# Loads on a second queue, a shorter warm-up, a later scale and earlier weight loads in a conditioned transformer block

## The chip, the cores and the metric

The kernel runs on one core of one Trainium2 chip. The metric is the device time of one execution in microseconds; a kernel's time is the median of its runs.

## The reference, cut to what matters

One block on 2048 tokens of width 640, all in float32. A conditioning vector `c` gives six modulation vectors (shift, scale and gate, for attention and for the MLP). The input is normalised and modulated, goes through linear attention with 32 heads of width 20, and is added back through a gate; the sum is normalised and modulated again, goes through an MLP of width 1728 with a squared ReLU, and is added back through the second gate.

```python
mod = (_silu(c) @ w_mod).reshape(c.shape[0], 6, 1, -1)
sa, ca, ga, sb, cb, gb = (mod[:, 0], mod[:, 1], mod[:, 2], mod[:, 3], mod[:, 4], mod[:, 5])
h = _layernorm(x, axis=-1) * (1 + ca) + sa
x = x + ga * _A_ref(h, A_wqkv, A_w_phi, A_wo)
h = _layernorm(x, axis=-1) * (1 + cb) + sb
x = x + gb * _B_ref(h, B_w1, B_b1, B_w2, B_b2)
...
# in _A_ref, per head: features are softmax(q w_phi) and softmax(-q w_phi), the same for k
o = num / den          # phi_q (phi_k^T v)  over  phi_q (phi_k^T 1)
# in _B_ref
r = jnp.where(h > zero, h, zero); h = r * r
```

## The kernel before, in words

**Numbers in two parts.** Every matmul operand is held as a high and a low part: ACT copies the value into a rounded format (the high part), DVE subtracts that from the value (the low part, `lo`, line 80), and `three` (line 76) makes three matmuls of each product. A weight therefore passes through three steps: a raw tile is loaded, ACT makes its high part, DVE its low part.

**The start.** The head matrices of `w_phi` lie in a block matrix `bd`. `fold` (line 231) multiplies the raw k and q weights by it, 12 matmul instructions for each of five pieces `d` of k and then of q. While the loads are under way, PE runs `WARM` matmuls on a tile of ones (lines 551 to 553); a float32 matmul is two instructions in the trace. The first two tokens' tiles (`XB[0]`) are normalised by `stats` and `scale`, transposed, modulated by `out0` (`t_out`, line 336: two ACT steps and one DVE step), and used by `k_step` (line 539), five steps `d` of 12 matmuls; `mod_rows2`, `mod_sb` and `mod_cols2` work out the modulation columns between them. Within this loop (lines 579 to 591) the next pair of tiles, `XB[1]`, gets its `stats` at `d == 1` and its `scale` (line 502, two ACT steps) at `d == 2`. After the loop ACT makes the high part of the first v weight (`v_hi(0)`) and empties the four PSUM banks of the k products (`to_sb`), which the q products then take.

**The middle.** For token tiles 2 to 13 the loop at line 641 makes k, q, v, the exponentials and the running k-v sums, with preparations (`side`) between. The q exponentials go out to DRAM and come back.

**The output projection and the preparation of the MLP.** Lines 1284 to 1332 run the first four pairs of token tiles through `do_wo`; the steps in `EXTRA` normalise the results (`ln2`), send them to DRAM in blocks (`blocks`, on ACT's queue, tile `xn`), bring them back (`back`, on SP's queue, tile `sb`) and transpose them on DVE (`turn`). The 28 MLP weight pieces stand in one list, `preps`, that runs through w1 and w2 by turns. Three counters go through it: `p_load` issues the raw load, `p_hi` is ACT's step and `p_lo` is DVE's. Nine loads are issued ahead of the MLP.

**The MLP.** `group(0)` to `group(3)` (line 1543) take 512 tokens each. Step `f` of 14 computes `up_mm` for piece `f` of w1, ACT's ReLU (line 1375) and square, both parts, and, two steps later, `down` with piece `f` of w2. In group 0 the weights are still being prepared: at step `f` PE does `up_mm(f)`; then come the low parts of the weights whose high parts came a step before; then the ReLU; then the normalisation of the next group's pairs 2 and 3 in pieces, with `back(2)` at step 5 and `back(3)` at step 7; then `p_hi` up to piece 2f+7; then `down(f - 2)`; and last `p_load` up to piece 2f+11. POOL and DVE meanwhile work on the late q tiles (`late_load`, `late_out`).

**What sets the order.** Between `manual_schedule` and its end, the engines named there (in this stretch PE, DVE and ACT) keep the order in which the program writes the instructions. SP's queue is not among them for this stretch: a planner puts SP's transfers in order by its own simulated clock, taking an instruction as soon as its inputs and a slot for its output are there, and the chip then runs that queue strictly in that order. `behind_sp` (line 1152) ties `back` to a place behind the last SP transfer that the program has written so far. The loop over tiles 2 to 13 is put in order by the planner on all engines.

**Slots.** Tiles with the same tag share a fixed number of slots (line 40). A tile gets its slot when its first writer is put in order, and tiles of one tag get theirs in the order in which the program writes their first writers. Raw pieces 0 to 8 are in tag `s1` (3 slots); later ones go by turns into `s1`, `s2` (2 slots) and `s4` (5 slots). The s4 slots were last held by the tiles `ept` of the output projection. One s4 slot goes to `LATE["b"]` (trace name `etl`), first written by `late_out(8)` at step 4 of group 0. The prepared pieces are in tag `w` (21 slots) or in the ring; the ring's 'w' slots for pieces 16 and 17 (w1 piece 9, w2 piece 7) were last held by the normalised tiles `xm` of pairs 2 and 3, which are free when `blocks` has written them to DRAM.

Of the kernel before, what the change touches and what calls it, by code (L numbers as in the profile page):

```python
# [22 lines left out]
NC = D // P  # L23
NF = 14
# [8 lines left out]
FIRST = 4  # L33
NTA = 2 * FIRST
RAWQ = NTA + 3
WARM = 14
APART = 256 + 16
SIDES = 3
DIRECT = range(6)
# [4 lines left out]
def kernel(  # L44
# [19 lines left out]
    nc = tc.nc  # L64
# [11 lines left out]
    def three(ah, al, bh, bl):  # L76
        return [(ah, bh), (ah, bl), (al, bh)]
# [16 lines left out]
    def tok2(tag, name):  # L94
        return mem.tile([P, 2, D], F32, tag=tag, name=name, bufs=BUFS[tag])

    def row(tag, name):
        return mem.tile([P, D], F32, tag=tag, name=name, bufs=BUFS[tag])
# [4 lines left out]
    def wslot(name, tag="w", pool=None):  # L103
        t = tok2(tag, name) if pool is None else pool.tile([P, 2, D], F32, tag=tag, name=name)
        return t.bitcast(F32R)
# [11 lines left out]
    def pj(name):  # L117
        return [psA.tile([P, 512], F32, tag="pj", name=f"{name}_{h}", bufs=4) for h in range(2)]

    def tp(name):  # L120
        return psA.tile([P, 512], F32, tag="tp", name=name)
# [16 lines left out]
    c_t = const.tile([P, NC], F32, name="c_t")  # L138
# [41 lines left out]
    first = tc.manual_schedule(engines={ET_.PE, ET_.DVE, ET_.Activation, ET_.Pool, ET_.SP})  # L180
    first.__enter__()

    nc.sync.dma_start(c_t, c)
    bd_t = row("s4", "bd_t")
    nc.sync.dma_start(bd_t, bd)
    raw, WM, RV, XB = {}, {}, {}, {}

    def load_raw(nm, w5, w1):
        raw[nm] = [tok2("w", f"raw_{nm}{i}") for i in range(3)]
        nc.sync.dma_start(raw[nm][2][:40, 1], w1)  # L190
        for d in range(NC):
            nc.sync.dma_start(raw[nm][d // 2][:, d % 2], w5[d * P : (d + 1) * P])

    def load_x(j):
        XB[j] = tok2("x", f"xb{j}")
        nc.sync.dma_start(XB[j], x[256 * j : 256 * j + 256].rearrange("(i p) d -> p i d", p=P))
# [31 lines left out]

    W = {}

    def fold(nm, d):

        w = wslot(f"w{nm}{d}")
        W[nm, d] = w
        p = pj(f"fold{nm}{d}")
# [132 lines left out]
    def proj(nm, t, cuts=((0, 320), (320, 640)), between=None):  # L368
# [3 lines left out]
        for h, (a, b) in enumerate(cuts):  # L372
# [3 lines left out]
            for d in range(NC):  # L376
                w = W[nm, d]
                terms += three(HT[j][:, d, 0, s], HT[j][:, d, 1, s], w[:, 0, a:b], w[:, 1, a:b])
# [144 lines left out]
    def mod_sb(d):  # L523
        t = MR[d, "sb"] = row("s1", f"msb{d}")[:, :P]
        nc.scalar.activation(t, MR[d][:, :P], AF.Identity, bias=plus[:, 0:1])
# [13 lines left out]
    def k_step(d):  # L539
        w = W["k", d]  # L540
        for t in range(2):
            s = slice(t * P, (t + 1) * P)
            for h in range(2):
                a, b = h * HALF, (h + 1) * HALF
                mm(PP[t][h][:, :HALF], three(HT[0][:, d, 0, s], HT[0][:, d, 1, s], w[:, 0, a:b], w[:, 1, a:b]),
                   first=(d == 0), last=(d == NC - 1))

    def out0(d):
        t_out(cols_a, HT[0], d, "a0", TR[d])

    warm = tp("warm")
    for i in range(WARM):
        nc.tensor.matmul(warm[:, :P], ones, ones, start=True, stop=True)
# [25 lines left out]
    for d in range(NC):  # L579
        if d + 1 < NC:  # L580
            mod_cols2(d + 1)
            out0(d + 1)
        if d + 2 < NC:
            mod_rows2(d + 2)
        k_step(d)
        if d + 2 < NC:
            mod_sb(d + 2)
        if d == 1:
            n1 = stats(XB[1], "a1")
        if d == 2:  # L590
            scale(XB[1], *n1)

    def v_hi(d):
        W["v", d] = wslot(f"wv{d}")
        nc.scalar.activation(W["v", d][:, 0], RV[d], AF.Copy)

# [266 lines left out]
    def late_exp():  # L863
        if "exp" in LATE:
            exps(ET[LATE.pop("exp")])
# [184 lines left out]

    W1, W2 = {}, {}

    def prep_load(k, f, w):
        n = FS[f]
        W = W1 if k == "1" else W2
        if k == "1":
            w = w.rearrange("p s (k n) -> p s k n", k=NC)
        W[f] = w
        i = preps.index((k, f))
        raw = row(("s1", "s2", "s4")[i % 3] if i > 8 else "s1", f"rw{k}_{f}")  # L1060
        if k == "1":
            raw = raw.rearrange("p (k n) -> p k n", k=NC)
        for r in range(P // n):
            if k == "1":
                nc.sync.dma_start(raw[:, :, r * n : r * n + n], w1[:, f * P : f * P + n].rearrange("(k p) n -> p k n", p=P))
            else:
                nc.sync.dma_start(raw[r * n : r * n + n], w2[f * P : f * P + n])
        RAW[k, f] = raw
# [1 line left out]
    RAW = {}  # L1070

    def prep_hi(k, f):
        w = (W1 if k == "1" else W2)[f]
        nc.scalar.activation(w[:, 0], RAW[k, f], AF.Copy)  # L1074

    def prep_lo(k, f):
# [18 lines left out]
    places = []  # L1095
    todo = {"load": list(preps), "hi": list(preps), "lo": list(preps)}

    def p_load(n=1):
        for _ in range(n):
            if todo["load"]:  # L1100
                k, f = todo["load"].pop(0)
                prep_load(k, f, places.pop(0)(f"w{k}_{f}"))

    def p_hi(n=1):
        for _ in range(n):
# [178 lines left out]
    for j in range(FIRST):  # L1284
        nxt = j + 1 < FIRST
        b, c = 2 * j + 5, 2 * j + 6
# [256 lines left out]
    def group(g):  # L1543
# [5 lines left out]
        for f in range(NF):  # L1549
            if nxt:  # L1550
                if f == 1 and not early:
                    load_x1(a)
                if f == 4 and not early:
                    load_x1(b)
                if f == (2 if early else 3):
                    lns.append([0, a, ln2(a)])
                if f == (4 if early else 7):
                    lns.append([0, b, ln2(b)])
                if f == 8:
                    fa_new()  # L1560
                    turn(a)
            if g == 0:
                if f == 0:
                    up_start(g, 2, 2)
                elif f > 1:
                    up_mm(g, f)
            elif g == FIRST // 2:
                if f == 0:
                    up_start(g, 4, 3)
                elif f == 2:  # L1570
                    up_mm(g, 4)
                elif f > 4:
                    up_mm(g, f)
            else:
                up_mm(g, f)
            if nxt and f == 11:
                turn(b)
                affine(range(NC))
            if f == (6 if g else 11):
                residual(g)  # L1580
            if f == 9 and g:
                add_b2(g)
            if g == 0:
                if f == 1:
                    late_slots()
                    for t in range(2):
                        late_load(NTA + t)
                    late_list()
                p_lo(len(todo["lo"]) - len(todo["hi"]))
                if 3 <= f < NF - 1:  # L1590
                    fill((3.5, 3.5, 3.5, 3.5, 3.0, 1.0, 0.0, 2.0, 1.0, 2.0)[f - 3])
            elif early:
                if f == 4:
                    late_blocks(4)
                    last_row("s1", 6)
                if f in (6, 7):
                    late_turn(4, ("q0", "q1") if f == 6 else None, LAST[4], (range(5), range(5, 11))[f - 6])
                if f == 8:
                    late_blocks(5)
                if f == 12:  # L1600
                    kv2_load()
                    late_wo(range(3))
                if f:
                    fill(3.4 if f in (6, 7, 9) else 5.2)
                if f == NF - 1:
                    assert not FILL, FILL
            if not more and f:
                round2(g, f)
            if f == 0 and g in (0, FIRST // 2):
                up_relu(g, 0)  # L1610
                up_relu(g, 1)
            if f == 2 and g == FIRST // 2:
                up_relu(g, 2)
                up_relu(g, 3)
            if g != FIRST // 2 or f != 3:
                up_out(g, f)
            if g == FIRST // 2 and f == 2:
                up_out(g, 3)
            if g and (more or f == 0):
                round2(g, f)  # L1620
            late_exp()
            for n in lns:
                n[0] += 1
                for _ in range(1 + (n[0] == 3)):
                    next(n[2], None)
                if n[0] == 4:
                    back(n[1])
            if g == 0:
                p_hi(2 * f + 7 - (2 * NF - len(todo["hi"])))
            if f == NF - 1 and nxt:  # L1630
                split2(range(NC))
            if f >= LAG:
                down(g, f - LAG)
            if g == 0:
                p_load(2 * f + 11 - (2 * NF - len(todo["load"])))
            else:
                ring_loads(g, f, FIRST // 2 if early else NGR)
        if g == 0:
# [94 lines left out]
```

## Time and profile before

| | us |
|---|---|
| median of 3 runs | 790.95 |
| lowest, highest run | 790.09, 791.35 |
| profiled execution | 790.26 |
| its span, first to last instruction | 788.6 |
| PE busy (matmul) | 777.0 |
| DVE busy | 553.8 |
| ACT busy | 403.0 |
| POOL busy | 76.5 |

Times in the trace count from the start of the span. In a timeline a row gives start and length in us, then engine, source line, operation, output and inputs, shape and count; the bracket gives the engine's idle time before the row and what ended it. A list of waits gives the total, the number of waits and the longest. SPq and ACTq are the issue of a DMA by that engine's queue; the transfer itself lands later. A table by windows gives, for each stretch, its length, the busy time of each engine with the number of instructions, then the granted clock, the busy share of the DMA engines and GB/s.

### The profile page before, as it was taken

The numbers are of one execution on the slowest core, as the hardware profiler recorded it, in microseconds if no ns is written. First come the engines' busy times: TensorE is split into PE (matmuls) and PEld (weight loads), VectorE is DVE, ScalarE is ACT, GpSimd is POOL, SyncE is SP. The second block draws the span as 40 slices with busy tenths as digits, with TensorE's granted clock in tenths as the row PEclk, the third lists the DMA queues.
The fourth block names the chain that finished last, engine by engine and source line by source line (L and its number), as shares of the span: only waits on it lengthen the run. The fifth ranks groups of instructions, "written<-read, shape, count | busy, mean of one in ns | idle before, by whom it ended". The sixth has DMA issues, their size and how long they took to land.

```text
span 788.6 us, 13327 instructions
## 1 busy us (share of the span) xinstructions
PE 777.0 (99%) x5171; PEld 717.4 (91%) x5171; DVE 553.8 (70%) x917; ACT 403.0 (51%) x789; POOL 76.5 (10%) x181
## 2 busy tenths in 40 slices
PE   9999999999999999999989999999999999999997
PEld 8899999999998988898979989999899999989997
DVE  4498999999766488664869699966945343575544
ACT  4667585655734344655938354531265644433221
POOL 3002020000000022201323000100010001000000
PEclk9999999999999999999999999999999999999999
DMA  8713248234121253567798747995779755145121
GB/s 329 265 36 132 101 163 278 90 140 152 54 84 34 84 185 137 167 188 243 245 350 293 249 165 265 282 330 201 206 234 343 274 169 166 51 150 200 34 84 67
DMA packets 76437, 142.31 MB, mean 180 GB/s; under 512 B 12718, under 2 KB 37422, under 8 KB 76374
## 3 DMA queue, kind: packets, MB, share of 16 engines
q1 hardware_dynamic: 69382, 117.74, 45.5%
q0 software_dynamic: 4096, 16.78, 5.6%
q10 hardware_dynamic: 2896, 6.94, 2.3%
q8 instruction: 40, 0.66, 0.3%
q14 instruction: 23, 0.19, 0.1%
HBM read 98.40 MB, written 42.93 MB: 179 GB/s over the span
## 4 chain that ended last, share of the span: by engine, by line
PE 80%; DVE 7%; DMA 5%; ACT 4%; POOL 2%; issue 1%; SPq 0%; ACTq 0%; DVEq 0%; POOLq 0%
PE up L70 20%; PE acc L70 13%; PE pv L70 9%; PE acr L70 8%; PE pk L70 8%; PE pq L70 8%; PE pwo L70 7%; PE kvp L415 3%; DMA xn<-xm 2%; DVE dn L813 2%; DVE scr L811 1%; DMA rw<-in_w 1%; DVE ezb L832 1%; PE ta L325 1%; DMA raw_k<-in_wk 1%
## 5 line engine op out<-in xcount | busy, mean ns | idle before, releaser
L70 PE MATMUL up<-h,w 128*128 128x512 f32 (+1 forms) x910 | 198.3, 371 | 2.9 <-ACT r L1375 2.7
L70 PEld LDWEIGHTS up<-h,w 128*128 128x128 f32 x910 | 155.7, 188 | 31.1 <-ACT r L1375 3.1
L70 PE MATMUL acc<-w,r2t 128*128 128x384 f32 x656 | 151.0, 336 | 0.1
L70 PE MATMUL acr<-w,r2t 128*128 128x256 f32 x656 | 112.8, 279 | 0.0
L70 PEld LDWEIGHTS acc<-w,r2t 128*128 128x128 f32 x656 | 107.5, 188 | 4.6 <-DVE r2t L80 0.4
L70 PEld LDWEIGHTS acr<-w,r2t 128*128 128x128 f32 x656 | 105.6, 188 | 0.0
L70 PE MATMUL pk<-wk,hT 128*128 128x320 f32 x480 | 79.8, 313 | 1.5 <-ACT hT L340 0.9
L70 PE MATMUL pwo<-wo,ot 128*128 128x320 f32 (+1 forms) x512 | 79.5, 313 | 0.1
L70 PE MATMUL pv<-wv,hT 128*128 128x360 f32 (+1 forms) x480 | 77.7, 311 | 0.0
L70 PEld LDWEIGHTS pwo<-wo,ot 128*128 128x128 f32 (+1 forms) x512 | 75.7, 188 | 1.1 <-DVE xm L1043 0.4
L70 PE MATMUL pq<-wq,hT 128*128 128x320 f32 x480 | 76.4, 314 | 0.1
L70 PEld LDWEIGHTS pk<-wk,hT 128*128 128x128 f32 x480 | 71.5, 188 | 3.7 <-ACT hT L340 1.4
L70 PEld LDWEIGHTS pv<-wv,hT 128*128 128x128 f32 x480 | 72.6, 188 | 0.3
L70 PEld LDWEIGHTS pq<-wq,hT 128*128 128x128 f32 x480 | 70.6, 188 | 1.6 <-ACT k L391 0.6
L1375 ACT ACTIVATE r<-up,b_t 128x512 f32<-128x512 f32 x52 | 35.0, 679 | 68.1 <-PE up L70 60.1
L80 DVE TENSOR_TENSOR r2t<-r,r2t 128x512 fp32r<-128x512 f32 (+1 forms) x56 | 38.4, 685 | 34.9 <-ACT r2t L1387 32.1
L80 DVE TENSOR_TENSOR w<-rw,w 128x640 fp32r<-128x640 f32 (+2 forms) x42 | 33.2, 814 | 28.3 <-ACT w L1074 16.9
L1386 DVE TENSOR_TENSOR r<-r 128x512 f32<-128x512 f32 x26 | 17.9, 690 | 47.1 <-ACT r L1375 47.1
L1387 ACT ACTIVATE r2t<-r 128x512 fp32r<-128x512 f32 x52 | 32.9, 633 | 22.4 <-DVE r L1386 21.6
L1477 ACT ACTIVATE w<-rw 128x640 fp32r<-128x640 f32 x42 | 30.6, 730 | 26.3 <-DVE rw L1476 24.1
L338 ACT ACTIVATE hfa<-ta,cols_a 128x256 f32<-128x256 f32 x30 | 17.0, 565 | 28.7 <-PE ta L325 28.6
L1074 ACT ACTIVATE w<-rw 128x640 fp32r<-128x640 f32 x28 | 19.4, 727 | 18.9 <-DMA xn<-xm 10.7
(241 smaller groups left out, 1079.7 us busy)
## 6 DMA issues: line engine op xcount, KB each, us to landing
rw<-in_w SPq DMA_DIRECT2D x65, 320.0 KB, 4.4
w<-w2d SPq DMA_DIRECT2D x28, 320.0 KB, 5.0
w<-w1d SPq DMA_DIRECT2D x12, 640.0 KB, 4.5
esp<-eq SPq DMA_DIRECT2D x11, 640.0 KB, 3.6
wm<-in_w_mod SPq DMA_DIRECT2D x20, 320.0 KB, 3.6
xb<-in_x SPq DMA_DIRECT2D x8, 640.0 KB, 4.1
el<-esp SPq DMA_DIRECT2D x8, 640.0 KB, 4.0
xx<-in_x SPq DMA_DIRECT2D x16, 320.0 KB, 3.5
```

What stands on the lines that cost most here:

```text
L70: nc.tensor.matmul(o, a, b, start=first and i == 0, stop=last and i == len(terms) - 1, skip_group_check=skip,)
L80: (eng or nc.vector).tensor_tensor(out_lo, full, hi.bitcast(F32), op=ALU.subtract)
L325: nc.tensor.transpose(p[:, i * P : (i + 1) * P], xn[:, i, d * P : (d + 1) * P], ident)
L338: nc.scalar.activation(hf, p[:, :256], AF.Identity, bias=cols[:, d : d + 1], scale=cols[:, 5 + d : 6 + d])
L415: nc.tensor.matmul(kvp[64 * c : 64 * c + 64, g // 4, a : a + 2 * n].rearrange("p (s n) -> p s n", s=2), v[:, u], e[:, :, o : o + n], start ...
L811: nc.vector.tensor_tensor(z, flat(ET[t]), flat(zb), op=ALU.mult)
L813: nc.vector.tensor_reduce(dn.rearrange("p s h -> p (s h)"), heads(z), axis=AX.X, op=ALU.add)
L1074: nc.scalar.activation(w[:, 0], RAW[k, f], AF.Copy)
L1375: nc.scalar.activation(r, UP[f], AF.Relu, bias=b1_t[:, f : f + 1])
L1386: nc.vector.tensor_tensor(r, r, r, op=ALU.mult)
L1387: nc.scalar.activation(t[:, 0], r, AF.Copy)
L1477: nc.scalar.activation(w[:, 0], raw, AF.Copy)
```

## The change

Five edits go in together. The block matrix and `c` are issued by ACT's queue, with `bd` first, and no longer by SP's. The small piece of raw k and q weights (`w1` in `load_raw`, 40 rows) goes behind the first large piece. Warm-up has ten matmuls for fourteen. `scale(XB[1])` moves from the end of step `d == 2` to the end of step `d == 3`. The prepared tile of an MLP piece is taken in `prep_hi` and no longer in `prep_load`, and in group 0 the raw loads are written up to piece 2f+15 instead of 2f+11.

```diff
-WARM = 14
+WARM = 10
...
-    nc.sync.dma_start(c_t, c)
     bd_t = row("s4", "bd_t")
-    nc.sync.dma_start(bd_t, bd)
+    nc.scalar.dma_start(bd_t, bd)
+    nc.scalar.dma_start(c_t, c)
...
         raw[nm] = [tok2("w", f"raw_{nm}{i}") for i in range(3)]
-        nc.sync.dma_start(raw[nm][2][:40, 1], w1)
         for d in range(NC):
             nc.sync.dma_start(raw[nm][d // 2][:, d % 2], w5[d * P : (d + 1) * P])
+            if d == 0:
+                nc.sync.dma_start(raw[nm][2][:40, 1], w1)
...
-        if d == 2:
+        if d == 3:
             scale(XB[1], *n1)
...
-    def prep_load(k, f, w):
+    def prep_load(k, f):
         n = FS[f]
-        W = W1 if k == "1" else W2
-        if k == "1":
-            w = w.rearrange("p s (k n) -> p s k n", k=NC)
-        W[f] = w
...
     def prep_hi(k, f):
-        w = (W1 if k == "1" else W2)[f]
+        w = places.pop(0)(f"w{k}_{f}")
+        if k == "1":
+            w = w.rearrange("p s (k n) -> p s k n", k=NC)
+        (W1 if k == "1" else W2)[f] = w
         nc.scalar.activation(w[:, 0], RAW[k, f], AF.Copy)
...
-                prep_load(k, f, places.pop(0)(f"w{k}_{f}"))
+                prep_load(k, f)
...
-                p_load(2 * f + 11 - (2 * NF - len(todo["load"])))
+                p_load(2 * f + 15 - (2 * NF - len(todo["load"])))
```

## The prediction

> **What bounds the kernel now.** I read the page's totals first, then the list of what each engine waits for, then the timeline at the places that the diff touches.
>
> ```profile
> span 788.6 us, 13327 instructions
> PE 777.0 (99%) x5171; PEld 717.4 (91%) x5171; DVE 553.8 (70%) x917; ACT 403.0 (51%) x789; POOL 76.5 (10%) x181
> ```
> ```profile
> PE up L70 <- ACT r L1375: 2.7, 2, 1.9
> ```
>
> PE is busy for 777.0 of 788.6 us and executes in order. The edits leave all matmuls but the warm-up alone, so a gain can come only from a warm-up that ends sooner or from one of PE's few waits. The largest entry of the list, up behind the ReLU (2.7 us in two waits, the longer 1.9), lies where the raw loads are moved; two smaller ones, in brackets in the rows of parts 1 and 2, are foldk and pk. A microsecond taken from PE there should arrive at the end, for PE has hardly any idle time later that could take it back.
>
> **Part 1: the start.** Timeline of the first 15 us:
>
> ```profile
> 0.81 0.39 SPq L183 DMA_DIRECT2D c_t<-in_c  x1
> ...
> 1.25 0.42 SPq L185 DMA_DIRECT2D bd_t<-in_bd  x1
> ...
> 2.18 2.25 SPq L192 DMA_DIRECT2D raw_k<-in_wk  x5
> ...
> 6.28 1.64 PE L241 MATMUL foldk<-bd_t,raw_k 120*128 120x120 f32 x12
> 7.17 0.47 ACT L248 ACTIVATE wk<-foldk 128x360 fp32r<-128x360 f32 x1 [4.04 <-PE foldk L241]
> 8.10 6.66 PE L241 MATMUL foldk<-bd_t,raw_k 120*128 120x120 f32 x48 [0.18 <-DMA raw_k<-in_wk]
> 12.30 0.87 DVE L494 BATCH_NORM_STATS2 sta<-xb 128x6 f32<-128x320 f32 x2
> ```
> The chain of waits has the second raw piece's transfer, and the view of the tile xb the time from issue to landing:
> ```profile
> 2.58 5.48 DMA raw_k<-in_wk
> ```
> ```profile
> DMA to landing us min/median/max: 7.6/7.6/7.6
> ```
> Busy time of line 553 by stretch (PE, PEld, granted clock, DMA share, GB/s):
> ```profile
> 1.00:5.27 4.27, 4.21 (x19) 4.21 (x20) 1.00 0.67 184
> 5.27:6.27 1.00, 1.00 (x11) 0.98 (x9) 1.00 0.94 261
> ```
>
> The 14 matmuls of the warm-up are 28 instructions. One takes 4.21/20 = 0.21 us up to 5.27 and about 1.00/9 = 0.11 us behind that: the first ten matmuls (20 instructions) run at half pace, the last four at full pace. Leaving out four removes the last eight, about 0.9 us. Fold k0 then starts near 5.3 instead of 6.28 if bd and raw_k0 have landed; both are issued earlier now, bd by ACT at about 0.8, raw_k0 by SP as its first transfer at 0.81 instead of 2.18 or so. The second fold is what counts: it starts at 8.10, with the landing of a piece issued at 2.58. On SP it loses c and bd ahead of it: the first piece and w1 remain, two issues instead of four, so it leaves at about 1.7, 0.86 earlier. The transfers themselves still carry bd, the first piece and w1 ahead of it, so the landing gains less than the issue; I estimate 0.45 (bd is no longer behind c, one issue interval, 1.25 - 0.81) to 0.86. Behind the folds stand the statistics of x: they run at 12.30, and x landed at 4.48 + 7.6 = 12.08 (the issue of x at 4.48 is the tail of SP's row of raw_k pieces, 2.18 + 2.25), so a gain there is again that of the transfers. I take 0.65, the middle. Upper end: fold k1 directly behind a k0 that runs 5.28 to 6.92, so 8.10 - 6.92 = 1.2. Lower end: 0, if the transfers go at the same bytes per second and x lands as before.
>
> On ACT two issues of about 0.4 us each now come first, and its first step on c correspondingly later; ACT next has work for PE at 7.17 (idle 4.04 before), which hides this. Without that cover it would be the 0.8 us of the issues.
>
> **Part 2: the scale one step later.** Timeline:
>
> ```profile
> 34.95 1.73 ACT L504 ACTIVATE xb<-xb,nba,sqa 128x640 f32<-128x640 f32 x2 [0.60 <-POOL nba L499]
> 35.00 0.16 DVE L530 TENSOR_REDUCE cols_a<-kvp 128x2 f32<-128x4 f32 x1 [0.45 <-PE kvp L529]
> ...
> 37.17 0.42 ACT L340 ACTIVATE hT<-hfa 128x256 fp32r<-128x256 f32 x1
> 37.49 0.72 ACT L595 ACTIVATE wv<-rawv 128x640 fp32r<-128x640 f32 x1
> 37.63 2.19 PE L70 MATMUL pk<-wk,hT 128*128 128x320 f32 x12 [0.91 <-ACT hT L340]
> 38.55 1.75 ACT L391 ACTIVATE k<-pk 128x320 f32<-128x320 f32 x4 [0.34 <-PE pk L70]
> 39.66 0.46 PE L70 MATMUL pq<-wq,hT 128*128 128x320 f32 x2
> ```
>
> `out0(4)` needs only the columns, ready at 35.16, but ACT is in the scale until 34.95 + 1.73 = 36.68: hT ends at 37.17 + 0.42 = 37.59 and PE waits 0.91. With the scale behind `out0(4)`, ACT begins it 1.5 sooner, hT is there near 36.1, and PE goes on at 37.63 - 0.91 = 36.72 with no wait. This removes 0.91. But the 1.73 us are not gone: they and wv's 0.72 now stand between hT and `to_sb`, whose first step frees the bank for pq. ACT would be through at 36.1 + 1.73 + 0.72, about 38.5, where the row of k stands now (38.55; PE's k step ends 0.9 earlier, at 38.9 instead of 39.8, with its first bank earlier than that). The first of the four k steps takes 1.75/4 = 0.44, so pq goes at about 38.9 to 39.0 and not at 39.66: 0.7 to 0.75. I take 0.75; the ends are 0.3 (the emptied bank comes as late as ACT's queue can make it, 0.45 more) and 0.91.
>
> **Part 3: raw loads written earlier.** Two waits of PE stand here:
>
> ```profile
> 369.69 0.74 ACT L1074 ACTIVATE w<-rw 128x640 fp32r<-128x640 f32 x1 [5.79 <-DMA rw<-in_w]
> ...
> 397.16 0.42 ACTq L1150 DMA_DIRECT2D xn<-xm  x1
> ...
> 407.81 1.36 ACT L1074 ACTIVATE w<-rw 128x640 fp32r<-128x640 f32 x2 [10.67 <-DMA xn<-xm]
> 409.08 0.67 ACT L1375 ACTIVATE r<-up,b_t 128x512 f32<-128x512 f32 x1
> ```
> ```profile
> 373.09 2.11 PE L70 MATMUL up<-h,w 128*128 128x512 f32 x8 [0.82 <-ACT r L1375]
> ...
> 409.80 2.57 PE L70 MATMUL up<-h,w 128*128 128x512 f32 x10 [1.88 <-ACT r L1375]
> ```
> SP's issues, and the DMA share by stretch (last three numbers: clock, share, GB/s):
> ```profile
> 335.90 0.47 SPq L1065 DMA_DIRECT2D rw<-in_w  x1
> 341.82 2.51 SPq L1161 DMA_DIRECT2D sb<-xn  x4
> ...
> 383.75 0.82 SPq L1067 DMA_DIRECT2D rw<-in_w  x2
> 384.61 0.45 SPq L1065 DMA_DIRECT2D rw<-in_w  x1
> ...
> 392.86 2.66 SPq L1161 DMA_DIRECT2D sb<-xn  x4
> 397.25 7.11 SPq L1065 DMA_DIRECT2D rw<-in_w  x3
> ```
> ```profile
> 396.00:400.00 4.00, 4.00 (x25) 3.71 (x24) 3.97 (x5) 1.13 (x2) 2.79 (x5) 1.00 1.12 327
> ```
>
> At 369.69 ACT waits for a raw piece. It lies in s1 or s2, whose next slot comes free only with the low part of an earlier piece; writing the load sooner does not free a slot, so the 0.82 stays. Taking the prepared tile in `prep_hi` moves nothing by itself: a slot is given at the first write, which stands in `prep_hi` both times.
>
> The s4 pieces differ. Two of them, w2 piece 7 and w1 piece 11, are written behind `etl` now, so they get its successor slots and go at 384. With four pieces more ahead they are written before step 4's `late_out(8)`, and the s4 slots of `ept` are free from about 336 (first s4 row, 335.90). They move to about 336, out of the stretch from 384 to 408 at whose busiest, from 396 to 400, the DMA engines are at share 1.12. What is late in that stretch is xn, issued at 397.16 and landed at 407.8, on which the high parts of pieces 16 and 17 wait 10.67 us on ACT, behind them the ReLU r (409.08) and PE (1.88). Each piece is 128 x 640 x 4 bytes, two are 0.66 MB, and at some 327 GB/s that is 2.0 us less ahead of xn, slightly more than the 1.88. `back(2)` helps as well: it was tied behind piece 18 and stood at 392.86, ahead of xn; it will be tied behind piece 22, in SP's row of 397.25 to 404.36. What is late next is r itself, which needs PE's up. I take 1.5, not all of it, because xn shares the queues with whatever moves up; ends 0 and 1.88.
>
> The price at the new place: two pieces at 336, 2.0 us of transfer, ahead of sb (341.82), whose turn on DVE
> ```profile
> 350.11 2.27 DVE L1171 STREAM_TRANSPOSE fa_q<-sb 128x256 f32<-128x256 f32 x4
> 413.83 2.23 DVE L1171 STREAM_TRANSPOSE fa_q<-sb 128x256 f32<-128x256 f32 x4
> ```
> comes at 350.11, 8.3 us behind the issue; without that slack DVE and then PE would lose up to 2.0. The later `back(2)` has its turn at 413.83, 9.5 us behind the end of SP's row; if it lands beyond, DVE stands in it and the low parts behind it come late.
>
> **Sum.** 0.65 + 0.75 + 1.5 = 2.9. The profiled execution took 790.26 (span 788.6 and 1.66 around it), 0.69 below the median of 790.95; its time would be 787.4, and on the median 788.0. The ends add to 0.3 and 4.0.
>
> **The rivals.** *A: the change to the raw loads does not do what it says*, since slots and not the text decide; for it speaks the wait at 369.69, against it that only s4 has an outside holder. Parts 1 and 2 remain: 790.95 - 1.4 = 789.55.
>
> *B: the start gains nothing*, x landing at 12.1 as before: 790.95 - 2.25 = 788.7. For it speaks the DMA share of 0.94 at 5.27 to 6.27; against it the 0.67 before.
>
> *C: the pace drops.* Full pace came at 5.27, just where the tenth warm-up ends. If it comes only after it, 24 fold instructions of 3.28/24 = 0.14 us (from 1.64 for 12) run at twice that for some 1.7 us: part 1 becomes 0.65 - 1.7 = -1.05, the time 789.75. The Trainium skill, "TensorE: Matmul & The Clock Gate", Part 1, bears on this: full rate is granted after a busy window of about 3.4 us whose start does not follow the first matmul. By that rule ten matmuls at half rate (4.2 us) do not always hold a whole window; the trace, with full pace after 4.2 us, agrees in the one case it shows.
>
> *D, slower: the planner puts tiles 2 to 13 in another order.* They are ordered by its simulated clock, and every input shifts.
> ```profile
> 239.46 1.49 DVE L406 TENSOR_REDUCE sk<-ek 128x64 f32<-128x1280 f32 x1 [1.54 <-ACT ek L402]
> 240.86 0.41 DVE L80 TENSOR_TENSOR hT<-hfa,hT 128x256 fp32r<-128x256 f32 x1
> 241.19 0.55 DVE L407 RECIPROCAL sk<-sk 128x64 f32<-128x64 f32 x1
> 241.77 1.49 DVE L408 TENSOR_TENSOR ek<-ek,sk 128x1280 f32<-128x1280 f32 x1
> ```
> If one such group (1.49 + 0.41 + 0.55 + 1.49 = 3.94) falls ahead of an hT that PE awaits, PE idles that long: 788.0 + 3.94 = 792.0. It decides once the new idle time exceeds 2.9. Against it: the present order is planned in the same way and has no such group ahead of PE, whose largest waits are the up's of 2.7.
>
> **How the numbers follow.** Forecast 0.46 (its own range 786.3 to 789.5), A 0.22, B 0.12, C 0.08, D 0.12. A difference of 0.2%, 1.58 us, is what this kernel's measurement can tell. Faster: the forecast, B and about a third of A and C, with the misses of the forecast off, 0.66; slower: D and little else, 0.13; the rest, 0.21, is within it. The range 785.6 to 791.2 holds all but D and leaves room for a start that gains more than 0.65.
>
> **What would show it.** Start: fold k1 at about 7.4 instead of 8.10, the statistics of x before 12.0, warm-up of 20 instructions. Scale: the row of xb behind hT, the pk wait of 0.91 gone, pq at about 0.75 less. Raw loads: two rw issues near 336 for those at 383.75 to 384.61, xn landing in under 9 us, ACT's wait of 10.67 shorter and the 1.88 gone, the 0.82 still there. Wrong would be: x landing no earlier, the 1.88 in place, a fold at over 0.14 us an instruction, or new PE idle time between 40 and 250.

## The result, and the profile after

| | before | changed |
|---|---|---|
| median of 6 runs, us | 791.15 | 786.35 |
| lowest, highest run | 790.09, 792.17 | 785.72, 787.05 |
| profiled execution | 790.26 | 786.04 |

The ratio is 0.994, with a 95% interval of 0.9927 to 0.9952: 4.8 us faster, where 2.9 was forecast. The two profiled executions differ by 4.22, and this is what the traces have to explain; the other 0.6 between the medians stands in no trace. Totals of the page, and what is left in the list of PE's waits:

```profile
span 784.3 us, 13311 instructions
PE 775.4 (99%) x5163; PEld 716.2 (91%) x5163; DVE 553.4 (71%) x917; ACT 402.7 (51%) x789; POOL 78.8 (10%) x181
```
```profile
PE up L70 <- ACT r L1375: 0.8, 1, 0.8
PE pq L70 <- ACT k L392: 0.4, 1, 0.4
...
PE foldq L242 <- DVE wk L80: 0.3, 1, 0.3
```

Of the up's 2.7 us 0.8 remain. Both waits of pk have left the list: the 0.9 behind ACT's hT, and one of 0.6 behind DVE's hT near 243. Two small waits are new: pq behind the copy of k, and fold q behind DVE's low part of a folded weight. Timeline of the start:

```profile
0.80 0.41 ACTq L184 DMA_DIRECT2D bd_t<-in_bd  x1
0.80 0.39 SPq L191 DMA_DIRECT2D raw_k<-in_wk  x1
...
1.06 4.33 PE L554 MATMUL warm<-ones 128*128 128x128 f32 x20 [1.06 <-POOL ones L129]
...
5.22 8.20 PE L242 MATMUL foldk<-bd_t,raw_k 120*128 120x120 f32 x60
...
11.12 0.89 DVE L495 BATCH_NORM_STATS2 sta<-xb 128x6 f32<-128x320 f32 x2
...
13.69 2.58 PE L242 MATMUL foldq<-bd_t,raw_q 120*128 120x120 f32 x18 [0.27 <-DVE wk L80]
```
The 60 fold instructions of k are one row: the second piece is there when it is wanted. The fold ends at 5.22 + 8.20 = 13.42 and not at 8.10 + 6.66 = 14.76, 1.34 earlier. The statistics of x run 1.18 earlier (11.12 for 12.30), and DVE makes the next low parts of the folded k weights behind them (DVE in the changed kernel, then in the kernel before):

```profile
13.16 1.63 DVE L80 TENSOR_TENSOR wk<-foldk,wk 128x360 fp32r<-128x360 f32 x4
```
```profile
14.33 1.63 DVE L80 TENSOR_TENSOR wk<-foldk,wk 128x360 fp32r<-128x360 f32 x4
```
In all 14 profiled executions fold q starts 0.05 to 0.06 us behind the end of the first of these low parts, here at 13.69 and before at 14.86. So 1.17 us are won at this place. They are the gain of the statistics and not the 1.34 of the fold, and PE waits 0.27.

Timeline of ACT and PE at the scale:

```profile
34.03 0.57 ACT L339 ACTIVATE hfa<-kvp,cols_a 128x256 f32<-128x256 f32 x1 [0.85 <-DVE cols_a L531]
34.62 0.42 ACT L341 ACTIVATE hT<-hfa 128x256 fp32r<-128x256 f32 x1
34.95 1.72 ACT L505 ACTIVATE xb<-xb,nba,sqa 128x640 f32<-128x640 f32 x2
36.58 0.72 ACT L596 ACTIVATE wv<-rawv 128x640 fp32r<-128x640 f32 x1
```
```profile
33.55 3.76 PE L70 MATMUL pk<-wk,hT 128*128 128x320 f32 x24
37.67 4.52 PE L70 MATMUL pq<-wq,hT 128*128 128x320 f32 x29 [0.36 <-ACT k L392]
```
The scale stands behind hT, and the fourth and fifth k steps are one row with no wait. Scale and wv then hold up the copy of k, and PE waits 0.36 for it. The q products start at 37.67 instead of 39.66, 1.99 earlier; 1.17 of this is the start, 0.82 the scale.

Timeline of the stretch around xn of pair 3, on SP, ACT, PE and DVE:

```profile
334.53 0.46 SPq L1064 DMA_DIRECT2D rw<-in_w  x1
335.10 2.11 SPq L1062 DMA_DIRECT2D rw<-in_w  x1
...
399.57 9.50 SPq L1161 DMA_DIRECT2D sb<-xn  x8
```
```profile
395.08 0.37 ACTq L1150 DMA_DIRECT2D xn<-xm  x1
401.37 1.37 ACT L1074 ACTIVATE w<-rw 128x640 fp32r<-128x640 f32 x2 [6.33 <-DMA xn<-xm]
```
```profile
371.20 3.72 PE L70 MATMUL up<-h,w 128*128 128x512 f32 x15 [0.79 <-ACT r L1375]
...
405.88 3.60 PE L70 MATMUL up<-h,w 128*128 128x512 f32 x15
409.31 0.69 PE L70 MATMUL acc<-w,r2t 128*128 128x384 f32 x3
```
```profile
411.62 2.23 DVE L1171 STREAM_TRANSPOSE fa_q<-sb 128x256 f32<-128x256 f32 x4 [4.14 <-DMA sb<-xn]
```
w2 piece 7 and w1 piece 11 are issued at 334.5 and 335.1. ACT's wait for xn has fallen from 10.67 to 6.33, and the up at 405.88 (409.80 before) has no wait. The 0.82 at 373 is still there with 0.79. In the kernel before, the acc behind the up at 409.80 held a second wait, inside its row, after DVE had waited for ACT's high parts (timelines of DVE and PE, kernel before):

```profile
408.58 1.56 DVE L80 TENSOR_TENSOR w<-rw,w 128x640 fp32r<-128x640 f32 x2 [6.33 <-ACT w L1074]
```
```profile
413.36 1.06 PE L70 MATMUL acc<-w,r2t 128*128 128x384 f32 x3
```
It took 1.06 us for three instructions and now takes 0.69. On DVE the turn of pair 2 waits 4.14 us for sb, which is now issued behind the last raw pieces; PE does not feel it here.

PE's lead over before, matmul by matmul: 1.17 at fold q, 1.99 at the q products, 1.37 at 200, 1.87 from 270 to 349, 1.88 at 371, 3.92 at the up of 405.88, 4.42 at the up after it, 4.26 at the end. The dip at 200 belongs to a new order: between 69 and 239 us 276 of PE's matmul records stand in another place than before. That goes with the scale: every kernel with the scale at step 3 has a new order there (best has 261 in another place), every one with it at step 2 has the order of before.

### The profile page after: what moved, and what is told of

The parts are those of the page before. It is cut to its first block, busy times and chain, and to the rows that moved or that the text cites. A ratio compares the mean times of both kernels' runs of the same rounds, so it can differ in the third digit from the quotient of the medians.

```text
span 784.3 us, 13311 instructions
## 1 busy us (share of the span) xinstructions
PE 775.4 (99%) x5163; PEld 716.2 (91%) x5163; DVE 553.4 (71%) x917; ACT 402.7 (51%) x789; POOL 78.8 (10%) x181
## 4 chain that ended last, share of the span: by engine, by line
PE 82%; DVE 7%; DMA 4%; ACT 3%; POOL 2%; issue 1%; SPq 0%; ACTq 0%; DVEq 0%; POOLq 0%
PE up L70 22%; PE acc L70 14%; PE acr L70 9%; PE pv L70 9%; PE pk L70 9%; PE pq L70 8%; PE pwo L70 4%; PE kvp L416 3%; DVE dn L814 2%; DVE scr L812 1%; DMA rw<-in_w 1%; PE ta L326 1%; DVE ezb L833 1%; DMA xb<-in_x 1%; DMA w<-w2d 1%
```

## The experiments

Each ratio is to the kernel before, run on the same chip between the others; intervals are 95%.

| kernel | median, us | before, us | ratio | interval |
|---|---|---|---|---|
| p1_start | 790.49 | 790.65 | 1.0002 | 0.9990 to 1.0015 |
| p1_warm | 790.64 | 790.65 | 0.9998 | 0.9988 to 1.0007 |
| p1_loads | 790.71 | 790.65 | 0.9997 | 0.9988 to 1.0005 |
| p2_scale | 790.11 | 790.65 | 0.9996 | 0.9984 to 1.0008 |
| p3_raw | 788.10 | 790.82 | 0.9958 | 0.9947 to 0.9970 |
| u_start | 786.99 | 790.82 | 0.9950 | 0.9938 to 0.9962 |
| u_scale | 787.05 | 790.82 | 0.9945 | 0.9933 to 0.9957 |
| u_ahead | 789.48 | 791.32 | 0.9977 | 0.9968 to 0.9986 |
| u_ahead_late | 787.49 | 791.32 | 0.9955 | 0.9942 to 0.9967 |
| u_back19 | 786.74 | 791.32 | 0.9945 | 0.9932 to 0.9958 |
| ahead19 | 786.89 | 791.32 | 0.9944 | 0.9932 to 0.9957 |
| best | 784.68 | 790.82 | 0.9927 | 0.9915 to 0.9940 |

### The start: both halves, and each alone

p1_start is the kernel before with the whole of part 1; p1_warm has the shorter warm-up alone, p1_loads the loads alone.

```diff
 p1_start, p1_warm
-WARM = 14
+WARM = 10
 p1_start, p1_loads
-    nc.sync.dma_start(c_t, c)
-    nc.sync.dma_start(bd_t, bd)
+    nc.scalar.dma_start(bd_t, bd)
+    nc.scalar.dma_start(c_t, c)
...
-        nc.sync.dma_start(raw[nm][2][:40, 1], w1)
...
+            if d == 0:
+                nc.sync.dma_start(raw[nm][2][:40, 1], w1)
```

> The kernel before with part 1 alone (block matrix and c on ACT's queue, w1 behind the first piece, ten warm-up matmuls). If the parts add up: fold q starts 1.17 us earlier than 14.86, as in the changed kernel, and the time falls by about 1.2 us, to 0.9985 of before. Rival, the gain of the start is taken back in the tiles that the planner orders: the fold is 1.2 early, the time stays within 0.3.

> The kernel before with ten warm-up matmuls for 14 and nothing else. Theory A, landings hold the start: the first fold piece lands at 6.10, the second at 8.06, so the first fold starts 0.1 to 0.2 earlier than 6.28 and the second at 8.10 as before; gain 0, ratio 1.000. Theory B, the warm-up holds it: first fold at 5.3, gain 0.6 or more. Theory C, the clock is granted later: fold instructions at more than 0.14 us each and a loss.

> The kernel before with the loads of part 1 and 14 warm-up matmuls. Theory A, landings hold the start: the pieces land 1.4 and 1.7 us earlier, so nothing but the warm-up is left; first fold at 6.28 as before, second without a wait at about 7.9, last fold of k ends near 14.5 instead of 14.76: gain 0.2 to 0.3, ratio 0.9997. Theory B, the warm-up holds it: no gain at all, since p1_warm has it. Theory D, each half of the change carries half: 0.6.

None of the three moves the time by what these runs can tell. On PE, in the profiled executions, fold q starts 0.44, 0.11 and 0.28 earlier than before. For the warm-up alone theory A holds: the second fold starts at 7.98, next to the 8.10 of before. For the loads the 0.2 to 0.3 came out, but by another way than written: the folds run 5.67 to 13.87, and fold q then waits 0.72 for DVE, whose statistics ran only at 12.01, because x landed at 11.99 (12.10 before).

Timeline rows of the warm-up and the fold, of p1_loads, of p3_raw (whose start is that of before) and of p1_start:

```profile
1.06 4.77 PE L554 MATMUL warm<-ones 128*128 128x128 f32 x28 [1.06 <-POOL ones L129]
5.67 8.20 PE L242 MATMUL foldk<-bd_t,raw_k 120*128 120x120 f32 x60
14.58 1.60 PE L242 MATMUL foldq<-bd_t,raw_q 120*128 120x120 f32 x11 [0.72 <-DVE wk L80]
```
```profile
1.06 6.24 PE L553 MATMUL warm<-ones 128*128 128x128 f32 x28 [1.06 <-POOL ones L129]
```
```profile
1.06 4.64 PE L554 MATMUL warm<-ones 128*128 128x128 f32 x20 [1.06 <-POOL ones L129]
5.49 8.82 PE L242 MATMUL foldk<-bd_t,raw_k 120*128 120x120 f32 x60
```
The same 28 instructions from the same start took 4.77, 5.39 (before) and 6.24 us: the step from half to full pace does not stand at a fixed point. In p1_start it came only within the fold, which took 8.82 and not 8.20. So rival C does happen in some executions, for 0.62 here and not for the 1.7 of its price, and part 1 has no single value.

Behind the start p1_start keeps 0.42 of its 0.44 up to 349 us and loses it in the first of the two up waits, 1.74 where before has 0.82; the second is as long as before (1.92 for 1.88):

```profile
373.66 2.57 PE L70 MATMUL up<-h,w 128*128 128x512 f32 x10 [1.74 <-ACT r L1376]
...
410.42 3.71 PE L70 MATMUL up<-h,w 128*128 128x512 f32 x15 [1.92 <-ACT r L1376]
```

### The scale alone

```diff
-        if d == 2:
+        if d == 3:
             scale(XB[1], *n1)
```

> The kernel before with the scale one step later and nothing else. Theory: the wait of 0.91 ahead of the fifth k step goes, a wait of about 0.35 ahead of the q products comes, net 0.8 on PE at 40 us, and the time falls by 0.8 to 790.3 where before is 791.1 (ratio 0.999). Rival: the wait moves whole to the q products, net 0.

In the trace the step is as expected: PE's lead changes from -0.28 (a late second raw piece) to 0.79 at the fifth k step and to 0.54 at the q products, net 0.82; at 349, behind the newly ordered stretch, 0.43 is left, net 0.71. The median falls by 0.5, less than these runs resolve.

### What made xn late: two pieces or the place of sb2

The change moved two things out of the way of xn: the two raw pieces, and sb2 (`back(2)`), which is tied behind the last transfer written. Four kernels take these apart: u_ahead has neither, u_ahead_late only the later sb2, u_back19 only the earlier pieces, the changed kernel both.

```diff
 u_ahead and u_ahead_late, against the changed kernel
-                p_load(2 * f + 15 - (2 * NF - len(todo["load"])))
+                p_load(2 * f + 11 - (2 * NF - len(todo["load"])))
 u_ahead_late as well
-                if n[0] == 4:
+                if n[0] == (6 if g == 0 and n[1] == 2 else 4):
                     back(n[1])
 u_back19, against the changed kernel (MARK[19]: the SP transfer of the 19th piece, index 18)
-        with behind_sp():
+        with tc.issue_after(MARK[19]) if j == 2 else behind_sp():
```

> The changed kernel with the raw loads again written up to piece 2f+11; the prepared tile is still taken in the high step. Theory: that edit alone moves nothing, the stall of PE near 406 is back with about 1.9 us and the small one behind it, and the time is 2.3 us above the changed kernel, 788.6 where that has 786.35 (ratio to before 0.997). Rival: the tile taken later frees a slot sooner and keeps a part of the gain.

> The kernel u_ahead with the call that brings pair 2 back (sb2) two steps later, so that SP issues it behind all of the raw pieces as in the changed kernel, while pieces 17 and 20 stay at 384. Theory P, the bytes of the two pieces made xn of pair 3 late: the stall is as in u_ahead, 788.6. Theory S, sb2 ahead of xn made it late: xn lands under 7.5 us behind its issue, no stall, 786.4. Both: about half, 787.5.

> The changed kernel with sb2 tied behind piece 18, as before the change, and not behind the last raw piece. Theory P, the bytes of the two pieces: xn of pair 3 still lands in 6 to 7 us, no stall, 786.4. Theory S, the place of sb2: xn lands in 9 us or more and PE waits 1 to 1.9 us near 406, 787.5 to 788.3.

ACT's wait behind xn in u_ahead, u_ahead_late and u_back19, and PE's up in the first two (the profile names rw in the second row, but xn lands at 405.03, just before ACT goes on):

```profile
407.27 1.36 ACT L1074 ACTIVATE w<-rw 128x640 fp32r<-128x640 f32 x2 [10.92 <-DMA xn<-xm]
...
409.26 3.73 PE L70 MATMUL up<-h,w 128*128 128x512 f32 x15 [2.40 <-ACT r L1375]
```
```profile
405.05 1.37 ACT L1074 ACTIVATE w<-rw 128x640 fp32r<-128x640 f32 x2 [9.31 <-DMA rw<-in_w]
...
407.04 3.73 PE L70 MATMUL up<-h,w 128*128 128x512 f32 x15 [0.68 <-ACT r L1375]
```
```profile
405.79 1.37 ACT L1074 ACTIVATE w<-rw 128x640 fp32r<-128x640 f32 x2 [8.79 <-DMA xn<-xm]
```

ACT's wait: 10.92 with neither, 9.31 with the later sb2, 8.79 with the earlier pieces, 6.33 with both. Each shortens it, by 1.6 and 2.1, and together by 4.6. The time does not add up in the same way: 1.8 us below before with neither, 3.8 and 4.6 with one, 4.8 with both. Theories P and S were put as opposites, and neither holds alone: both the pieces and sb2 make xn late, and moving both takes 0.9 more from ACT's wait than the two moves singly. Once xn is early enough for PE, the rest of the gain has no taker. The medians of u_back19 and the changed kernel, 0.4 apart, speak for such a limit. The profile of u_back19 has no wait at this up either, though xn lands only 2.1 us sooner after its issue than in u_ahead (8.73 for 10.87), but it is a weak witness: that execution, 789.0, is the slowest of its six. PE waited 1.95 at the earlier up, ran at half clock behind that (last section), and so came late to this one. That the prepared tile is taken later does nothing: u_ahead has that edit, and its stall is back with 2.40.

u_ahead, the first two parts without the third, is 1.8 us faster than before (1.1 to 2.5 by its interval), which leaves 3.0 to the changed kernel where 2.3 was expected.

### The raw loads alone, and even earlier

p3_raw is the kernel before with both edits of part 3; ahead19 is the changed kernel with `2 * f + 19`.

> The kernel before with part 3 alone. Theory, the stall near 408 goes whole and the small one behind it: 1.9 to 2.3 us below before, ratio 0.997 to 0.9976, and xn of pair 3 lands 6 to 7 us behind its issue. Rival, part 3 is worth more only where parts 1 and 2 bring PE to this place earlier: 1.5 or less here.

> The changed kernel with raw loads written up to piece 2f+19, which brings one more s4 piece to 335. Theory: PE has no wait left that hangs on it (0.8 near 370 hangs on an s1/s2 piece), so the time stays within 0.2 of the changed kernel, 786.35. Rival, the bytes at 335 come too dear: xn of pair 1 and sb1 late, DVE's turn near 348 waits and the time rises by up to 1 us. Rival, more is better: down by 0.5 or more.

Part 3 alone is worth 2.7 us by the medians and 2.4 to 4.2 by the ratio's interval: more than expected, and the larger part of the whole. xn lands 6.93 behind its issue, as expected. A new wait took back some of it in the profile. Timeline of DVE and PE in p3_raw:

```profile
414.81 2.28 DVE L1170 STREAM_TRANSPOSE fa_q<-sb 128x256 f32<-128x256 f32 x4 [4.19 <-DMA sb<-xn]
...
419.65 0.44 PE L70 MATMUL acc<-w,r2t 128*128 128x384 f32 x1 [0.39 <-DVE r2t L80]
```
DVE stands in the turn of pair 2 until sb2 has landed, its low parts come late, and PE waits; its lead falls from 1.94 to 1.31 here. u_start has the same with 0.41. In the changed kernel DVE waits as long without PE noticing. ahead19 is 4.4 us below before, not distinguishable from the changed kernel, which speaks for the first theory. It does not isolate the third piece, though: in its trace sb2 goes at 388.32, ahead of xn again, and xn lands 7.31 behind its issue where the changed kernel has 6.27, still early enough for PE.

### Part 1 and part 2 taken back

u_start is the changed kernel with SP's order and 14 warm-ups of before, u_scale with the scale at step 2.

> The changed kernel with part 1 taken back (block matrix and c on SP's queue, w1 first, 14 warm-up matmuls). Alone, part 1 brought PE 0.4 us forward and the time nothing. Theory, its gain is taken back only by the late transfers at 370 and 407, of which the second is gone in the changed kernel: 0.6 to 1.2 us above the changed kernel, 787.0 to 787.5. Rival, part 1 is worth nothing anywhere behind the first 350 us: 786.35 as the changed kernel.

> The changed kernel with the scale at step 2 again. Theory: the wait of 0.9 ahead of the fifth k step is back, the 0.36 ahead of the q products is gone, and the wait on DVE's hT near 243 (0.56 before) is back in whole or part; 0.8 us above the changed kernel, 787.1. Rival: nothing, 786.35.

Both medians are 0.6 to 0.7 above the changed kernel's, which was timed apart from them, as expected; but all three intervals overlap, so timing alone doesn't confirm either part. The traces do better for the scale. Waits of PE in u_scale:

```profile
PE pk L70 <- ACT hT L341: 0.9, 1, 0.9
...
PE pk L70 <- DVE hT L80: 0.6, 1, 0.6
```
The 0.9 is back, and with it the 0.6 near 243, which the list of the changed kernel does not have. (This execution, 785.37, is the fastest of its five; its fold q began 1.52 earlier than before.)

### A faster version

best is the changed kernel with the first v weight prepared behind the copies of k, and one high part less at step 1 of group 0:

```diff
-    v_hi(0)
-    v_lo(0)
     for t in range(2):
         PK[t] = row("s2", f"k{t}")
         to_sb(PP[t], PK[t])
-    for d in range(1, NC):
+    for d in range(NC):
         v_hi(d)
...
     exps(EK[0])
+    v_lo(0)
     v_lo(1)
...
-                p_hi(2 * f + 7 - (2 * NF - len(todo["hi"])))
+                p_hi(2 * f + (6 if f == 1 else 7) - (2 * NF - len(todo["hi"])))
```

> The changed kernel with two more moves: ACT and DVE make the parts of the first v weight behind the k products' copies and not ahead of them, and at step 1 of group 0 ACT makes one high part less (up to piece 8), so that the ReLU of step 2 no longer stands behind the high part of a piece that lands late. Theory: the waits of 0.36 (q products) and 0.8 (up near 370) go, 1.1 us below the changed kernel, 785.2, ratio to before 0.9926. Rival: the delayed parts free their raw slots later and PE waits for a later piece instead, 786.4 or more.

At 784.68 it is 6.1 us below before and has the lowest ratio of all, 0.9927. Its interval reaches to 0.994, so that it beats the changed kernel is likely but not settled. Timeline of ACT:

```profile
368.33 0.74 ACT L1073 ACTIVATE w<-rw 128x640 fp32r<-128x640 f32 x1 [5.95 <-DMA rw<-in_w]
368.97 0.67 ACT L1374 ACTIVATE r<-up,b_t 128x512 f32<-128x512 f32 x1
```
The ReLU follows the first late piece and no longer the second, and the up wait at 371 is gone: PE's lead grows from 1.71 to 2.67 here. The other edit gained 0.26 at the q products. In the stretch that the planner orders PE then meets a new wait of 0.60 for the copy of k at 130.74 and the wait on DVE's hT near 243 again, 0.56: the lead is 2.12 at the q products and 1.71 at 270. That edit is worth nothing by the trace.

## Why the prediction was right, point by point

**Direction and mechanism.** All three parts do on PE what the working said, the time lies in the range, and it fell by 4.8 us where 2.9 was forecast. That is more than the 4.0 to which the upper ends add. The range held it partly by luck: its extra room was meant for the start, while most of the excess came from part 3. The shortfall is in the sizes of two terms.

**Part 1, 0.65 taken, 1.17 in this trace.** The step that failed is "the landing gains less than the issue". The fold of k ran without a wait behind the warm-up, at the upper end that was given as 1.2. The second piece was issued 0.88 earlier (1.70 for 2.58) and landed 1.71 earlier (6.35 for 8.06); x was even issued 0.42 later (4.90 for 4.48) and landed 1.00 earlier (11.10 for 12.10). Why they landed that much earlier wasn't tested on its own. That the statistics of x stand behind the folds, and so pass on the gain of the transfers, was right. The value is not a constant: over the eight profiled executions with the new start, fold q began 0.43 to 1.52 earlier than in the profile of before, 0.94 in the mean; over the four with the old start, it began between 0.39 earlier and 0.58 later, 0.12 later in the mean. The difference, 1.06, is my best estimate for PE at 14 us. What of it arrives at the end isn't resolved: nothing with part 1 alone, 0.6 between the medians of u_start and the changed kernel.

**Part 2, 0.75 taken, 0.82 in this trace.** Wait, cover and what comes late next (the copy of k ahead of q) were as worked out. Behind the newly ordered stretch 0.70 of it is left (1.87 - 1.17).

**Part 3, 1.5 taken, 2.0 at the up and some 0.5 behind it.** Two terms were mis-sized. The bytes of the two pieces and the place of sb2 were not "2.0 us less" with a little help: the first took 2.1 from ACT's wait, the second 1.6, both 4.6. And the upper end of 1.88 left out a second victim of the late xn: DVE's low parts of pieces 16 and 17 waited 6.33 behind ACT's high parts, and the acc at 413.36, whose r2t stands behind them on DVE, lost 0.4 to 0.5 with them. With both added the lead grows by 2.5. What was said of the first stall (it stays, slots decide), of the prepared tile (moves nothing alone) and of the two pieces (to about 336) held. The price at the new place wasn't paid: the lead is 1.87 at 349 and 1.88 at 371.

**A microsecond taken from PE arrives at the end.** This is the assumption that the runs weaken. Between a gain at 14 us and the end lie two waits on transfers, near 372 and 408, and their length varied between profiled executions by more than the gain: 0.75 to 2.2 us for the first one wherever it was there. With one profile of each kernel, what is the kernel's and what the execution's can't be told apart in general; but the first wait was 1.03 to 2.2 in all four kernels with one particular order of transfers (last section), and p1_start and p1_loads are among them. That is where part 1 alone lost its gain in the profile.

**Rivals.** A fell: the loads do move. B fell here, where the statistics run at 11.12, but all but came in p1_loads (12.01). C did not happen in the profile after, and did in others (8.82 for the fold in p1_start). Its price doesn't fit its own count: 24 instructions at twice 0.14 lose 3.3 us and not 1.7.

Half of D came true: the planner did put the tiles in another order. The loss did not come: the lead fell from 1.99 at the q products to 1.37 at 200 and rose again to 1.87, so the stretch cost 0.12. The argument against D misread the profile. It said that no such group stands ahead of PE, but the group of its own rows does, for 0.56 (DVE and PE, kernel before):

```profile
243.18 0.85 DVE L80 TENSOR_TENSOR hT<-hfa,hT 128x256 fp32r<-128x256 f32 x2
```
```profile
243.66 2.61 PE L70 MATMUL pk<-wk,hT 128*128 128x320 f32 x16 [0.56 <-DVE hT L80]
```
In the changed kernel DVE comes to the last step of this group 2.39 earlier (239.38 for 241.77), more than PE's lead, and the wait is gone. In best PE does wait in this stretch, 0.60 and 0.56.

The slack that was claimed for sb2's turn was not there: DVE waits 4.14 for it. In two kernels PE waits 0.4 with it, and its lead falls by 0.6 to 0.7.

## What to carry to other kernels

A late transfer that everyone waits for can have several causes ahead of it in the queues, so list those transfers and move each alone and all together; but count the gain only up to the point where the waiting engine is next held by something else. Before a saving early in the program is counted at the end, look for waits on transfers further on, for they can grow by as much as was saved. Follow a late tile to its second and third user: here a high part on ACT held a low part on DVE, and this cost PE again 4 us later. Where a planner orders a stretch, an edit ahead of it can change the order of all of it, so compare the order before and after.

## What was not expected of the hardware

**The step to full pace moves.** In 14 profiled executions, all with the first matmul at 1.05 or 1.06 us and matmuls following without a long gap, it came between 3.97 and 7.14 us (read from where the starts of single instructions go from 0.21 to 0.11 us apart), that is 2.9 to 6.1 behind the first one. The Trainium skill, "TensorE: Matmul & The Clock Gate", Part 1, says that the window of about 3.4 us runs free and the step therefore varies by about 500 ns. The traces agree that it varies, but by 3.2 us, and in the earliest case it came before 3.4 us of matmuls had passed; for this kernel the measurement decides. Ten warm-ups or fourteen is thus a trade that differs from run to run.

**A wait can cost the clock as well.** In the profile of u_back19 PE waited 1.95 at the first up, and the up behind that took 5.30 us for 15 instructions, where the kernel before has 3.72. The granted clock (third number from the end of the second row) is 0.50 there:

```profile
373.15 5.30 PE L70 MATMUL up<-h,w 128*128 128x512 f32 x15 [1.95 <-ACT r L1377]
```
```profile
374.40:377.80 3.40, 3.40 (x9) 2.64 (x8) 1.97 (x3) 3.37 (x9) 0.38 (x2) 0.50 0.37 98
```
PE's lead over before fell by 1.56 in this up, on top of the wait. None of the other 13 profiles has such a stretch in the middle, though p1_loads waits 2.21 here and p1_warm 2.46 near 408. One difference is in the records: the full clock of u_back19 lasted from 5.74 to 374.38, which is 108 times 3.413 us, and in all 14 traces it lasted a whole number of times 3.413. The wait of u_back19 lay whole within one such stretch; of the other waits at most 1.75 us did (before, near 408). This is one case, and the rule wasn't tested.

**A third of a microsecond of order, one of wait.** Near 358 SP issues a raw piece, then x, then raw pieces, while POOL issues two loads of late_e. In before x follows the piece after 0.49, in p1_start after 0.80:

```profile
358.57 0.38 SPq L1065 DMA_DIRECT2D rw<-in_w  x1
...
359.06 0.45 SPq L1045 DMA_DIRECT2D x<-xm  x1
```
```profile
358.19 0.38 SPq L1066 DMA_DIRECT2D rw<-in_w  x1
...
358.99 0.33 SPq L1046 DMA_DIRECT2D x<-xm  x1
```
The next raw piece is issued 0.10 us after POOL's first late_e in before and lands ahead of it; in p1_start it is issued 0.29 after and lands behind it, 8.3 us behind its own issue and not 6.2. The raw piece after that, for which ACT waits near 370, lands 9.02 behind its issue and not 7.59, and PE waits 1.74 and not 0.82. All profiles fall into these two groups. In the four kernels with the late x (p1_start, p1_loads, u_ahead, u_ahead_late) that piece took 8.3 to 9.5 us, and the first up wait was 1.03 to 2.2. In the ten with the early x it took 7.3 to 8.0, and the wait was at most some 1.2, but for u_back19 with 1.95, where a load of POOL itself landed late. The four are just the kernels with the new loads of the start and raw loads up to 2f+11, so the order goes with the program. What in it delays x wasn't found, and no run changes this alone.
